# Sinkhorn attention and a residual MLP in one kernel: a later place for the mixed values of batch 1, their round trip through another queue, and several small operations moved

## The chip, the core and the metric

The kernel runs on one core of a Trainium2 chip. The metric is the device time of one execution in microseconds. A core has five engines that run side by side, each through its own list of instructions in order: TensorE (PE, matrix products into PSUM), VectorE (DVE), ScalarE (ACT), GpSimd (POOL) and SyncE (SP), which here only issues DMAs. An instruction waits on semaphores for what it needs; everything behind it on its engine waits too. POOL also issues DMAs. PSUM is handed out in two pools: `psA`, two buffers of two banks, and `psB`, four buffers of one bank.

## What is computed

Inputs are q, k, v of 4 batches, 8 heads, 768 positions and 64 features, a small 8x8 matrix per batch and head, and the MLP's weights. The reference, cut to what matters:

```python
for _ in range(5):                               # on the 8x8 matrices P
    P = softmax over rows; P = P / column sums
k_sorted = einsum("bhij,bhjcd->bhicd", P, k_b)   # k, v cut into 8 blocks of 96 positions
v_sorted = einsum("bhij,bhjcd->bhicd", P, v_b)
attn = softmax(q_b @ k_sorted_b.T / 8)           # each block of q against its own mixed block
x = attn @ v_sorted_b                            # as [4, 768, 512]
a1 = alpha1 * x + beta1
u = x + lam * (w_tok @ a1)                       # mixes positions
a2 = alpha2 * u + beta2
out = u + lam * (relu(a2 @ w_ch1) @ w_ch2)       # 512 -> 2048 -> 512
```

## The kernel before

**Order by hand.** Every instruction of the five engines is issued through a wrapper (line 65), so that the profile shows L65 for nearly all, and groups are told apart by tile names. The program order of each engine is the order in which the Python code runs. The main part walks over 4 batches and 2 halves of positions (hf 0, 1). A half has an h part and a c part. The h part has 16 units `h_unit` (four products into one `psB` bank `h_ps`, then a relu on ScalarE into `hTa` or `hTb`). The c part of batch 0 has three `ch_unit`s of 16 products into one `psB` bank `ch_ps`, each in four parts, then VectorE's sum with u and two stores by SyncE; later batches use `ch_pair`, which saves products by adding and subtracting blocks (`sums`, `TWa`, `TWb`). After each h unit and each c part a table `at` is looked up: `put(batch, half, "h" or "c", n, f)` hangs f behind unit or part n. "h9" of half (0, 0) means: behind the tenth unit. Two entries at one place run in the order in which they were put.

**Work hung there for the next batch.** While batch b goes through the MLP, attention of batch b+1 is done in such places:

- `mix_matrix(b)` (line 371) builds the mixing matrices from P: one small product into a bank `repv_ps` and seven small VectorE operations.
- `mix_v(b, n)` mixes a third of the raw values: two products into a `psA` buffer (`mix_ps`), one ScalarE copy into `mixed`. `bounce_v(b)` writes `mixed` to a DRAM scratch `vscr` with two DMAs, `back_v(b)` reads it back turned, on SyncE, into `Vs`, which the products with the attention weights use.
- `mix_k(b, n)` mixes a third of the keys: eight products into `psA` (`kmix_ps`), four ScalarE copies into `kT`.
- `q_turn_late(g)` turns the queries of head pair g of batch 1: 24 small products into two `psB` banks (`q_ps`), one copy into `qT` from each bank.
- `score(b, g, hf)` forms scores in a `psA` buffer (`sc_ps`) and their exp on ScalarE (`et`); `pv` multiplies with the values into a `psA` buffer (`x_ps`), which VectorE divides and writes to `x`.
- `moe_tok(b, kt)` is the product over positions (`tok_ps`, in `psB`), VectorE adds into `u`, ScalarE copies to `u16`. `moe_cross(b, hf)` turns `u16` by three DMA transposes on SyncE into `uT`, and `moe_affine(b, hf)` makes the input `a2T` of the h part from it with four operations, on VectorE in batch 0.
- `block_weights(n)` makes one eighth of the weight differences `TWa`, `TWb` on VectorE, needed from batch 1 on.
- `block_sums` makes the `sums` on VectorE. `scale_weights` scales the second weight matrix there.

**The start.** Up to about 33 us batch 0's attention and the token weights are prepared. `slow(n)` (line 227) issues n dummy products in fp32 on zeros, whose result nobody reads. One stands at line 961 between `pv_first(0)` and `k_turn(0, 2)`. Loads with a change of type go through POOL in the order of the program: the weights W1p and W2p, then raw v, raw k and q of batch 1 (`load_kv`, `load_q`, line 988). `loads(2)` starts on POOL with a small copy `gate` that waits until `back_v(1)` has written `Vs`.

**Lines that the change touches:** 372 (`mix_matrix`), 541 (`q_turn_late`), 589 (`bounce_v`), 961 (`slow`), 1006 to 1008 (`mix_matrix`, `moe_cross`), 1019 to 1024 (batch 1), 1041 to 1046 (scores and pv of batches 2 and 3), 1064 (`block_weights`).

Of the kernel before, what the change touches and what calls it, by code (L numbers as in the profile page):

```python
# [16 lines left out]
def kernel(  # L17
# [56 lines left out]
    dve = Engine(nc.vector)  # L74
    act = Engine(nc.scalar)
    pool = Engine(nc.gpsimd)
    sp = Engine(nc.sync)
# [9 lines left out]
    def psa(shape, dtype, name):  # L87
        return pools["psA"].tile(shape, dtype, name=name, tag="psA")
# [138 lines left out]
    def slow(n, ps=psa):  # L227
        z = wz[:].bitcast(FT)
        out = ps([128, 512], FT, "warm_ps")
        for _ in range(n):  # L230
            pe.matmul(out[:], z[:, 0:128], z.unsqueeze(1).to_broadcast([128, 2, 256]), start=True, stop=True)
# [27 lines left out]
    def q_copy(b, g, ps, half, eng):  # L259
        eng(  # L260
            qT_of[b][:, g, :].rearrange("p (r t) -> p r t", t=12)[:, :, half * 6:half * 6 + 6],
            ps[half].rearrange("p (t r) -> p r t", t=6),
        )
# [83 lines left out]
    def mix_values(b, ps):  # L347
        bank = ps([128, 512], FT, "repv_ps")
        rep = bank[:, 0:NB * NB]
        pe.matmul(  # L350
            rep, ebh[:, b, :, :, :].rearrange("p a h j -> p (a h j)"),
            P16[:].rearrange("p i j -> p (i j)"), start=True, stop=True,
        )
        sel = att.tile([128, NB, NB], FT, name="sel", tag="sel", bufs=2)
        dve.tensor_tensor(
            sel[:], rep.rearrange("p (i j) -> p i j", j=NB),
            mlo[:].unsqueeze(1).to_broadcast([128, NB, NB]), ALU.mult,
        )
        red = bank[:, 64:64 + NB]
        dve.tensor_reduce(red, sel[:], AXX, ALU.add)  # L360
        big = att.tile([128, H, NB], F16, name="bigV", tag="bigV", bufs=2)
        dve.tensor_tensor(
            big[:], mhi[:].unsqueeze(2).to_broadcast([128, H, NB]),
            red.unsqueeze(1).to_broadcast([128, H, NB]), ALU.mult,
        )
        bigV[b] = big
# [2 lines left out]
    bigP = {}  # L369

    def mix_matrix(b):
        mix_values(b, psa)
        big = att.tile([128, 2, H * NB], F16, name="bigM", tag="bigM", bufs=3)
        dve.tensor_tensor(
            big[:], bigV[b][:].rearrange("p h i -> p (h i)").unsqueeze(1).to_broadcast([128, 2, H * NB]),
            mth[:].unsqueeze(2).to_broadcast([128, 2, H * NB]), ALU.mult,
        )
        bigM[b] = big
        bgp = att.tile([128, 2, 2, H4, NB], F16, name="bigP", tag="bigP", bufs=3)
        for th in range(2):  # L380
            dve.tensor_tensor(
                bgp[:, :, th, :, :], bigV[b][:].rearrange("p (g a) i -> p a g i", a=2),
                mth[:, th:th + 1].unsqueeze(2).unsqueeze(3).to_broadcast([128, 2, H4, NB]), ALU.mult,
            )
        bigP[b] = bgp
# [152 lines left out]
    def q_turn_late(g):  # L538
        ps = q_turn(1, g, psb)
        q_copy(1, g, ps, 0, dve.tensor_copy)  # L540
        q_copy(1, g, ps, 1, act.copy)

    gate = const([1, 1], F16, "gate")

# [7 lines left out]
    def mix_v(b, n, eng):  # L552
        if n == 0:
            mixed[b] = att.tile([128, HB, D], F16, name="mixed", tag="qn" if b == B - 1 else "sums", bufs=1 if b == B - 1 else 2)
        ps = psa([128, 2, 512], FT, "mix_ps")
        raw = raw_of[(b, 1)][:].rearrange("p t d -> p (t d)")
        for m in range(2):
            pe.matmul(
                ps[:, m, :], bigM[b][:].rearrange("p a x -> p (a x)"),
                raw[:, n * 1024 + m * 512:n * 1024 + (m + 1) * 512], start=True, stop=True,  # L560
            )
        eng(
            mixed[b][:, n * 16:(n + 1) * 16, :].rearrange("p t d -> p (t d)"),
            ps[:].rearrange("p m f -> p (m f)"),
        )
# [20 lines left out]

    def bounce_v(b):
        for th in range(2):
            pool.dma_start(
                vscr[b, :, th * HB:(th + 1) * HB, :], mixed[b][th * 64:(th + 1) * 64, :, :],  # L590
            )

    def back_v(b):
        sp.dma_start(Vs[0:BLK, :, 0:D], vscr[b].rearrange("x t d -> t x d"))
# [137 lines left out]
    def moe_cross(b, hf):  # L732
        uT = uT_of[(b, hf)] = att.tile([128, CT, 384], F16, name="uT", tag="uT", bufs=2)
        for m in range(3):
            sp.dma_start_transpose(
                uT[:, :, m * 128:(m + 1) * 128], u16_of[b][:, 3 * hf + m, :],
            )
# [220 lines left out]
    moe_start(0)  # L958
    a1_of[0] = moep.tile([128, 8, C], F16, name="a1", tag="a1", bufs=1)
    pv_first(0)  # L960
    slow(1)
    kp2 = k_turn(0, 2, psb)
    kp3 = k_turn(0, 3, psb)
    for g, kp in ((2, kp2), (3, kp3)):
# [29 lines left out]
    def put(b, hf, kind, n, *todo):  # L994
        at.setdefault((b, hf, kind, n), []).extend(todo)
# [7 lines left out]
    for ks in range(NT):  # L1003
        put(0, 0, "h", ks, lambda ks=ks: prep_wtok(ks, 1, psa, (dve.tensor_copy, act.copy)[ks % 2]))
    put(0, 0, "h", 6, lambda: mix_matrix(1))
    put(0, 0, "c", 6, lambda: mix_matrix(2))
    put(0, 0, "c", 7, lambda: mix_matrix(3))
    put(0, 0, "h", 9, lambda: moe_cross(0, 1))
    for g in range(CT):
        put(0, 0, "h", g, lambda g=g: first_affine(0, slice(0, 128), slice(0, NT), slice(g * 128, (g + 1) * 128)))  # L1010
    for m in range(3):
# [3 lines left out]
    for b in range(1, B):  # L1015
        p = b - 1
        if b == 1:
            for n in range(3):
                put(0, 0, "h", 11 + n, lambda n=n: mix_v(1, n, act.copy))
                put(0, 0, "c", 3 + 3 * n, lambda n=n: mix_k(1, n, (act.copy,) * 4))  # L1020
            put(0, 0, "h", 13, lambda: bounce_v(1))
            put(0, 0, "c", 1, lambda: back_v(1))
            for g in range(H4):
                put(0, 0, "c", (5, 7, 8, 10)[g], lambda g=g: q_turn_late(g))
            put(0, 0, "c", 11, lambda: loads(2))
            seq = [("s", 0), ("s", 1), ("s", 2), ("p", 0), ("s", 3), ("p", 1), ("p", 2), ("s", 4), ("p", 3), ("s", 5),
                   ("p", 4), ("s", 6), ("p", 5), ("s", 7), ("p", 6), ("p", 7)]
            for at_, (kind, n) in enumerate(seq):
                put(0, 1, "h", at_, (lambda n=n: score(1, n // 2, n % 2, psa)) if kind == "s" else (lambda n=n: pv(1, n // 2, n % 2)))
        else:  # L1030
            for n in range(3):
                put(p - 1, 1, "c", (n if b == 2 else 1 + n), lambda b=b, n=n: mix_v(b, n, act.copy))
            for n in range(3):
                put(p - 1, 1, "c", ((2, 5, 7), (4, 7, 10))[b - 2][n], lambda b=b, n=n: mix_k(b, n, (act.copy,) * 4))
            put(p - 1, 1, "c", b, lambda b=b: bounce_v(b))
            put(p - 1, 1, "c", (4 if b == 2 else 7), lambda b=b: back_v(b))
            for kt in range(NT):
                put(*((0, 1, "h", 13) if b == 2 else (1, 0, "c", 1)), lambda b=b, kt=kt: q_cross(b, kt))
            if b + 1 < B:
                put(p, 0, "h", 3, lambda b=b: loads(b + 1))  # L1040
            for (kind, n), at_ in zip(
                pairs, ((0, "h", 0), (0, "h", 2), (0, "h", 4), (0, "h", 6), (0, "h", 9), (0, "c", 0), (0, "c", 4), (1, "h", 2)),
            ):
                for i in range(2):
                    f = (lambda b=b, n=n + i: score(b, n // 2, n % 2, psa)) if kind == "s" else (lambda b=b, n=n + i: pv(b, n // 2, n % 2))
                    put(p, *at_, f)
            for at_ in ((0, "h", 5), (0, "h", 6), (0, "h", 10), (0, "h", 11), (1, "h", 0), (1, "h", 1), (1, "h", 3), (1, "h", 4)):
                put(p, *at_, flush_one)
        if b == 1:
            put(p, 1, "h", 15, flush)  # L1050
        put(p, 1, "h", 3, lambda b=b: moe_start(b))
        for kt in range(3):
            put(p, 1, *(("c", 3) if b == 1 else ("h", 9 + 2 * kt)), lambda b=b, kt=kt: moe_tok(b, kt, psb))
        put(p, 1, *(("c", 3) if b == 1 else ("h", 13)), lambda b=b: moe_cross(b, 0))
        for ci in range(CT):
            put(p, 1, "c", 8 if b == 1 else 8 + ci, lambda b=b, ci=ci: moe_affine(b, 0, (ci,)))
        for kt in range(3):
            put(b, 0, "h", 2 * kt, lambda b=b, kt=kt: moe_tok(b, 3 + kt, psb))
        put(b, 0, "h", 4, lambda b=b: moe_cross(b, 1))
        put(b, 0, "c", 2, lambda b=b: moe_affine(b, 1))  # L1060

    for g, m in enumerate((10, 11, 12, 12)):
        put(0, 0, "h", m, lambda g=g: scale_weights(g))
    for n, at_ in enumerate(((0, 1, "c", 7),) * 4 + ((0, 1, "c", 9),) * 4):
        put(*at_, lambda n=n: block_weights(n))
    for b in range(1, B):
        for hf in range(2):
# [66 lines left out]
```

## Time and profile before

| what | us |
| --- | --- |
| median of 3 runs (lowest to highest) | 259.27 (258.84 to 259.41) |
| the profiled execution | 259.36 |
| its span, first to last instruction | 257.6 |
| PE busy | 244.5 |
| DVE busy | 171.8 |
| ACT busy | 157.0 |
| POOL busy | 47.2 |

A busy TensorE is not TensorE at its peak: the ends of its products are modelled. In a timeline row stand the start, the duration, the engine, the operation, what is written from what, the shape, the number of instructions merged, and in brackets the idle time before, with what ended it. Rows of SyncE are issues; a DMA lands later.

The stages of TensorE in this execution: the h part of half (0, 0) ends at 54.9, its c part at 70.4; the h part of half (0, 1) ends at 86.0; the h part of batch 1 begins at 102.9, that of batch 2 at 158.6, that of batch 3 at 210.7.

### The profile page before, as it was taken

Reading aid. Unit: us, or ns where it says so; the run is one execution under the profiler, and the core shown is the slowest. Engines: PE = TensorE matmul, PEld = TensorE weight load, DVE = VectorE, ACT = ScalarE, POOL = GpSimd, SP = SyncE. Lnnn points to the kernel's source line nnn. Section 1 sums busy time; section 2 is a strip of 40 time slices with the busy share of each in tenths; the row PEclk is TensorE's granted clock in tenths of the full one; section 3 lists DMA queues with packets and bytes.
Section 4 is the critical chain, followed back from the end, with each engine's and each line's share of the span. In section 5 each row is a group of like instructions: output and inputs, shape, how many; then the busy total and the mean of one; then the engine's idle time right before and its main releaser. Section 6 shows DMA issues by size and latency. Waiting matters only on the chain.

```text
span 257.6 us, 6061 instructions
## 1 busy us (share of the span) xinstructions
PE 244.5 (95%) x2418; PEld 158.9 (62%) x2418; DVE 171.8 (67%) x457; ACT 157.0 (61%) x289; POOL 47.2 (18%) x72
## 2 busy tenths in 40 slices
PE   6789999899899999999999999999999999999993
PEld 2366665455455545456865787557756875686783
DVE  5694587654639955759896775298887863462773
ACT  4697675467798688496655587877465004837400
POOL 8598804010091010082000010000000000000000
PEclk9999999999999999999999999999999999999999
DMA  5999999997989976989991259910302232111023
GB/s 92 190 211 208 208 204 210 215 158 182 182 168 182 143 171 125 175 155 175 150 136 46 43 152 133 167 23 0 84 0 45 61 103 63 20 41 43 0 84 81
DMA packets 61936, 31.09 MB, mean 121 GB/s; under 512 B 50562, under 2 KB 57618, under 8 KB 61908
## 3 DMA queue, kind: packets, MB, share of 16 engines
q0 software_dynamic: 21136, 17.70, 44.5%
q1 hardware_dynamic: 40676, 12.97, 30.6%
q8 instruction: 19, 0.31, 0.5%
q14 instruction: 9, 0.07, 0.1%
q10 hardware_dynamic: 96, 0.03, 0.1%
HBM read 32.79 MB, written 8.65 MB: 161 GB/s over the span
## 4 chain that ended last, share of the span: by engine, by line
PE 66%; DMA 15%; DVE 10%; POOL 3%; issue 2%; ACT 2%; DVEq 0%; POOLq 0%
PE h_ps L65 26%; PE tok_ps L65 8%; PE px L65 8%; DMA raw<-in_v_dram 7%; PE ch_ps L65 6%; PE pz L65 5%; PE py L65 5%; DMA W1p<-in_moe_w_ch_dram 5%; DMA v<-in_v_dram 3%; DVE x L65 2%; PE x_ps L65 2%; PE sc_ps L65 2%; DVE ost L65 2%; DVE sums L65 2%; PE mix_ps L65 2%
## 5 line engine op out<-in xcount | busy, mean ns | idle before, releaser
L65 PE MATMUL h_ps<-a2T,W1p 128*128 128x384 bf16 x512 | 93.3, 326 | 0.3 <-DVE a2T L65 0.3
L65 PEld LDWEIGHTS <-W1p 128*128 128x128 bf16 x512 | 47.9, 98 | 31.3 <-issue 0.2
L65 ACT ACTIVATE hTa<-h_ps 128x384 f16<-128x384 f32 x64 | 31.3, 492 | 30.5 <-PE h_ps L65 29.3
L65 ACT ACTIVATE hTb<-h_ps 128x384 f16<-128x384 f32 x64 | 31.2, 490 | 7.5 <-PE h_ps L65 7.5
L65 DVE SCALAR_TENSOR_TENSOR u<-tok_ps,x 128x512 f32<-128x512 f32 x21 | 14.5, 691 | 25.5 <-PE tok_ps L65 25.5
L65 PE MATMUL tok_ps<-a,w_tokT 128*128 128x512 f16 x126 | 30.3, 379 | 0.0
L65 ACT CAST kT<-kmix_ps 64x512 f16<-64x512 f32 x36 | 25.7, 714 | 6.4 <-PE kmix_ps L65 5.9
L65 ACT CAST u<-u 128x512 f16<-128x512 f32 x21 | 13.0, 618 | 21.3 <-DVE u L65 21.2
L65 ACT ACTIVATE et<-sc_ps 96x768 f16<-96x768 f32 (+2 forms) x36 | 24.6, 743 | 1.7 <-PE sc_ps L65 1.7
L65 PEld LDWEIGHTS <-sums 128*128 128x128 f16 x216 | 21.1, 98 | 3.7 <-issue 0.6
L65 PEld LDWEIGHTS <-hTa 128*128 128x128 f16 x192 | 18.3, 98 | 6.7
L65 PEld LDWEIGHTS <-hTb 128*128 128x128 f16 x200 | 18.4, 98 | 5.9
L65 PEld LDWEIGHTS <-w_tokT 128*128 128x128 f16 x126 | 12.3, 98 | 13.1 <-issue 0.2
L65 DVE TENSOR_TENSOR x<-x_ps,rcb 96x512 f16<-96x512 f32 x24 | 16.5, 687 | 0.8
L65 DVE TENSOR_TENSOR sums<-hTa,hTb 128x512 f16<-128x512 f16 (+2 forms) x27 | 8.9, 330 | 10.3 <-ACT hTb L65 10.0
L65 PEld LDWEIGHTS <-et 96*128 96x128 f16 (+4 forms) x288 | 12.0, 100 | 2.6
L65 DVE SCALAR_TENSOR_TENSOR ost<-px,u 128x256 f32<-128x256 f32 x27 | 11.3, 417 | 3.4 <-PE px L65 3.4
L65 POOL DMA_DIRECT2D vscr<-mixed x6 | 3.3, 556 | 55.9 <-ACT mixed L65 55.9
L65 PE MATMUL x_ps<-Vs,et 96*128 96x65 f16 (+4 forms) x288 | 12.8, 195 | 0.0
L65 ACT CAST mixed<-mix_ps 128x1024 f16<-128x1024 f32 x9 | 9.1, 1013 | 5.3 <-PE mix_ps L65 5.2
L65 PE MATMUL ch_ps<-W2p,hTb 128*128 128x512 f16 x48 | 11.8, 379 | 0.0
L65 PE MATMUL ch_ps<-W2p,hTa 128*128 128x512 f16 x48 | 11.7, 379 | 0.0
(140 smaller groups left out, 360.9 us busy)
## 6 DMA issues: line engine op xcount, KB each, us to landing
out_dram<-ost SPq DMA_DIRECT2D x23, 192.0 KB, 2.7
raw<-in_v_dram POOLq DMA_DIRECT2D x6, 384.0 KB, 6.7
raw<-in_k_dram POOLq DMA_DIRECT2D x6, 384.0 KB, 9.7
vscr<-mixed POOLq DMA_DIRECT2D x6, 384.0 KB, 6.1
Vs<-vscr SPq DMA_DIRECT2D x3, 768.0 KB, 8.2
W1p<-in_moe_w_ch_dram POOLq DMA_DIRECT2D x4, 512.0 KB, 11.1
W2p<-in_moe_w_ch_dram POOLq DMA_DIRECT2D x4, 512.0 KB, 14.6
qn<-in_q_dram POOLq DMA_DIRECT2D x12, 128.0 KB, 11.1
```

The costliest lines, as they stand in the source:

```text
L65: ins = getattr(self.eng, name)(*args, **kwargs)
```

## The change

Seven edits.

1. The dummy product `slow(1)` at line 961 is taken out.
2. The mixed values of batch 1: `mix_v(1, n)` goes from h11, h12, h13 to h13, h14, h15 of half (0, 0), `bounce_v(1)` from h13 to h15, `back_v(1)` from c1 to c2.
3. `bounce_v(1)` is issued by SyncE instead of POOL (batches 2 and 3 stay on POOL). `moe_cross(0, 1)`, which is on SyncE too, goes from h9 to c0 and so stands behind the bounce.
4. Both copies of a late q turn are on VectorE (one was on ScalarE), and the four turns go from c5, c7, c8, c10 to c4, c5, c7, c8.
5. `mix_matrix` takes its bank from `psB` instead of `psA`. For batches 2 and 3 it goes from c6 and c7 of half (0, 0) to h1 and h2 of half (0, 1).
6. `block_weights` goes from c7 (four) and c9 (four) of half (0, 1) to c4 (three), c5 (three) and c6 (two).
7. Where two scores of batches 2 and 3 hang behind one h unit, the second goes one unit further. Scores that hang in the c part, and all `pv`, stay.

```diff
     def mix_matrix(b):
-        mix_values(b, psa)
+        mix_values(b, psb)
...
         q_copy(1, g, ps, 0, dve.tensor_copy)
-        q_copy(1, g, ps, 1, act.copy)
+        q_copy(1, g, ps, 1, dve.tensor_copy)
...
     def bounce_v(b):
         for th in range(2):
-            pool.dma_start(
+            (sp if b == 1 else pool).dma_start(
...
     pv_first(0)
-    slow(1)
     kp2 = k_turn(0, 2, psb)
...
-    put(0, 0, "c", 6, lambda: mix_matrix(2))
-    put(0, 0, "c", 7, lambda: mix_matrix(3))
-    put(0, 0, "h", 9, lambda: moe_cross(0, 1))
+    put(0, 1, "h", 1, lambda: mix_matrix(2))
+    put(0, 1, "h", 2, lambda: mix_matrix(3))
+    put(0, 0, "c", 0, lambda: moe_cross(0, 1))
...
-                put(0, 0, "h", 11 + n, lambda n=n: mix_v(1, n, act.copy))
+                put(0, 0, "h", 13 + n, lambda n=n: mix_v(1, n, act.copy))
...
-            put(0, 0, "h", 13, lambda: bounce_v(1))
-            put(0, 0, "c", 1, lambda: back_v(1))
+            put(0, 0, "h", 15, lambda: bounce_v(1))
+            put(0, 0, "c", 2, lambda: back_v(1))
             for g in range(H4):
-                put(0, 0, "c", (5, 7, 8, 10)[g], lambda g=g: q_turn_late(g))
+                put(0, 0, "c", (4, 5, 7, 8)[g], lambda g=g: q_turn_late(g))
...
+                split = kind == "s" and at_[1] == "h"
                 for i in range(2):
...
-                    put(p, *at_, f)
+                    put(p, *at_[:2], at_[2] + (i if split else 0), f)
...
-    for n, at_ in enumerate(((0, 1, "c", 7),) * 4 + ((0, 1, "c", 9),) * 4):
+    for n, at_ in enumerate(((0, 1, "c", 4),) * 3 + ((0, 1, "c", 5),) * 3 + ((0, 1, "c", 6),) * 2):
         put(*at_, lambda n=n: block_weights(n))
```

## The prediction

> **What bounds the kernel now.** I read the page's busy shares, then TensorE's waits, then the timelines around each wait.
>
> ```profile
> PE 244.5 (95%) x2418; PEld 158.9 (62%) x2418; DVE 171.8 (67%) x457; ACT 157.0 (61%) x289; POOL 47.2 (18%) x72
> ...
> PEclk9999999999999999999999999999999999999999
> ```
>
> TensorE is busy 244.5 of 257.6 us at the full granted clock, so a saving must either remove TensorE work or close one of its gaps. The list of what TensorE waited for (left out: five waits of the start, and 0.3 at 33.91 that no edit touches):
>
> ```profile
> PE mix_ps L65 <- DMA raw<-in_v_dram: 1.1, 1, 1.1
> PE q_ps L65 <- ACT qT L65: 1.0, 1, 1.0
> PE sc_ps L65 <- DVE x L65: 0.7, 2, 0.4
> ...
> PE sc_ps L65 <- ACT et L65: 0.5, 2, 0.3
> PE sc_ps L65 <- DVE kT L65: 0.4, 1, 0.4
> ...
> PE px L65 <- DVE ost L65: 0.2, 1, 0.2
> ```
>
> Read: waiter, releaser, us in total, times, longest. Together 3.9 us. The timelines place them (start, duration, in brackets the idle before):
>
> ```profile
> 20.66 1.47 PE L65 MATMUL warm_ps<-wz 128*128 128x512 f32 x2
> 22.07 0.94 PE L65 MATMUL k_ps<-bigK,k 64*64 64x64 f16 x48
> 23.40 0.52 PE L65 MATMUL sc_ps<-qT,kT 64*128 64x96 f16 x16 [0.39 <-DVE kT L65]
> ...
> 50.54 0.60 PE L65 MATMUL mix_ps<-raw,bigM 128*128 128x512 f16 x2 [1.09 <-DMA raw<-in_v_dram]
> ...
> 66.30 0.57 PE L65 MATMUL q_ps<-ident,q8b 64*64 64x64 f16 x24 [1.01 <-ACT qT L65]
> ```
>
> The profiled execution took 259.36 us: span 257.6 and 1.76 around it; it lies 0.09 above the median of the runs, 259.27. Sums below are made against 259.36.
>
> **1. slow(1) removed.** The dummy product holds TensorE from 20.66 to 22.07. Without it `k_turn(0, 2)` starts at about 20.7 and `k_turn(0, 3)` ends near 21.9 (its second bank is free when the exp that ends at 21.41 is done). The next score needs VectorE's `k_copy`, and VectorE is in the `x` product of `pv_first(0)` from 21.04 to 22.00. So that copy starts at 22.00 instead of 22.70, and the score at 22.7 instead of 23.40: 0.70 of the 1.41 us is gained, and TensorE idles 0.8 instead of 0.39. Up to 49 us everything on TensorE, VectorE and ScalarE follows in order; the weights do not hold it (the first W1p piece is issued at 19.0 and takes 10.0, to 29.0; its user, `h_ps` at 33.13, moves to 32.4).
>
> **2. Values of batch 1 two units later (h11..13 to h13..15).** The second raw v load is issued at 31.78 and takes 18.7 us: it lands at 50.50. The DMA engines move 200 to 217 GB/s throughout, so I leave that time where it is. TensorE had finished its earlier work at 49.45; less 0.70 that is 48.75. It now does h12 (0.65), `first_back(2)` (0.43) and h13 (0.65) first, up to 50.48, so it meets the landing within 0.1. After that come three mixes (0.43 each) and two units: 2.6, so the channel products start at 53.13 instead of 54.89. **Gain 1.76**: 1.09 of wait and 0.67 of part 1. Without part 1 it would be 1.09.
>
> **3. Bounce on SyncE, transposes behind it.** ScalarE's three `mixed` copies (1.01 each, with a 0.37 relu between) end at 55.02 before. They start from the same 50.5 and end at about 55.0 again, since ScalarE paces them. So the bounce leaves no earlier than its old 55.31. What changes is SyncE's queue: `moe_cross(0, 1)` is now behind it.
>
> ```profile
> 52.09 3.91 SPq L65 DMA_TRANSPOSE uT<-u  x3
> 62.50 0.36 SPq L65 DMA_DIRECT2D Vs<-vscr  x1
> ...
> 94.59 3.57 SPq L65 DMA_TRANSPOSE uT<-u  x1
> ```
>
> Two issues of about 0.4 (the `Vs` row; POOL's took 0.55) put the transposes at 56.1, 57.4 and 58.7, at their old pitch of 1.3: 4.0 us later than before. Call T the landing of the last. Neither a bounce on SyncE nor a transpose behind one is in this trace, so bounds: low, 58.7 + 2.4, the least landing of a `uT` transpose, 61.1; high, the first issue is held 3.57 as at 94.59, where stores and a bounce were in flight, and the landing is the largest, 4.2: 65.3. I take the median landing on the page, 4.0: **T = 62.7**.
>
> Who waits: `moe_affine(0, 1)` at c6 is first in VectorE's list there, ahead of the sum of channel unit 1 and both copies of q group 2. TensorE is not affected by c4 and c5. But q group 3 at c8 needs two of four banks; unit 2 holds one, so one must come back from group 2. From T: four affines 1.16, the sum 0.60, one copy 0.55 = 2.31. TensorE reaches c8 at 53.13 + nine parts of 0.865 + two key mixes of 0.45 + three turns of 0.50 + some 0.3 in changes between them = 63.6. **New wait: 62.7 + 2.31 - 63.6 = 1.4**; 0 at the low bound, 4.0 at the high one. In the kernel before, the transposes hid under loads and landed long before 63.63, where the affines started without a wait: that cover is what is given up.
>
> The Trainium skill, page "DMA: Bandwidth & Descriptors", section "Two DMAs through the same engine are not ordered", says that within one queue of a DMA engine descriptors start in order. That speaks against this edit: the transposes' data would start only behind the bounce's. By the same page's fit of 2.0 us plus bytes over 436 GB/s the 768 KB bounce would drain by about 59.1 (an estimate), three transposes at the 1.3 pitch would end at 63.0, and the sum would be 257.4 instead of 257.1; no run so far shows the bounce on SyncE.
>
> `back_v` stands behind the transposes (issued up to 59.9) and waits for the bounce: at POOL's 4.1 to 6.5 it goes at 60 to 62, not later than the old 62.50. It takes 8.2, so V is there by 70.2; the first `pv` (74.26 before) needs it at about 72.5. `loads(2)`, gated on it, is no later either. POOL loses two issues of 0.55; nobody waits for them.
>
> **4. q copies on VectorE, at c4, c5, c7, c8.** The old wait at 66.30 is for ScalarE's copy at 65.76, stuck behind four key casts:
>
> ```profile
> 62.86 2.88 ACT L65 CAST kT<-kmix_ps 64x512 f16<-64x512 f32 x4 [0.50 <-PE kmix_ps L65]
> 65.76 0.48 ACT L65 CAST qT<-q_ps 128x384 f16<-128x384 f32 x1
> ```
>
> **It goes: -1.01.** Four copies of 0.55 join VectorE, which has long idle stretches there (3.31 before 58.60, 1.95 before 61.24). Group 0 is needed at 57.9, its load lands at 41.9 + 14.1 = 56.0; groups 2 and 3 land at 58.2, needed at 62. If the bounce beside them delays these by its own 2 us, it still fits.
>
> **5. mix_matrix: psb, and batches 2 and 3 at h1, h2 of the next half.** The same TensorE work (0.13 each), moved. Its seven small VectorE operations (some 1.4 us each time) fall into VectorE's idle 3.38 before 74.72. Zero; if that cover were gone, 0.1 to 0.3.
>
> **6. Differences (block_weights) at c4 to c6.** Eight subtractions, 4.9 us, stood between the channel sums:
>
> ```profile
> 105.80 0.68 DVE L65 SCALAR_TENSOR_TENSOR ost<-ch_ps,u 128x512 f32<-128x512 f32 x1
> 106.40 0.68 DVE L65 SCALAR_TENSOR_TENSOR u<-tok_ps,x 128x512 f32<-128x512 f32 x1
> ...
> 107.12 0.62 ACT L65 CAST u<-u 128x512 f16<-128x512 f32 x1 [2.67 <-DVE u L65]
> 107.64 1.50 ACT L65 ACTIVATE et<-sc_ps 96x768 f16<-96x768 f32 x2
> ```
>
> The token sum ran at 106.40 though its product ended at 105.0; ScalarE idled 2.67 and its exps were late: TensorE's 0.20 and 0.35 (page: 0.5). They now fill VectorE's idle 3.21 before 99.22; the sum runs at once. **Gain 0.55.** Late next: the sum at 99.22 by 1.7, for which only a store waits.
>
> **7. Second scores one unit behind.** The two waits of 0.36 (114.69, 169.42) are for a bank that VectorE frees; a unit of 0.65 covers them. At 169 I count 0.30. At 114 nothing: VectorE is busy without a gap from 112.27 to 124.84, and TensorE already waits 0.21 for it at 124.89; that wait would grow instead. **Gain 0.30.**
>
> **Sum:** 259.36 - 1.76 - 1.01 + 1.4 - 0.55 - 0.30 = **257.1**.
>
> **Rivals.**
> A. No new wait: T at 61.1. For it: by 58.2 the loads are over, so transposes meet less traffic than at 52 to 58. 257.1 - 1.4 = 255.7. It holds up to T = 61.3.
> B. Slower: the transposes don't move until the bounce has landed. Place: SyncE's queue at 55.3. Price: a bounce landing of 6.5 (its largest row) after the second issue at 55.7 is 62.2; three transposes in 3.91 give T = 66.1, a wait of 4.8, and 260.5. For it: the 3.57 row. Against it: there, engines were full of other traffic too. It turns slower from T = 64.9, where the wait eats the 3.62 gained.
> C. The change does less than it says: part 1 gives nothing (a bank or `x` comes later than I read), or group 3 gets both banks of group 2 (one more copy, 0.5). 257.1 + 0.67 to 1.2 = 257.8 to 258.3.
>
> **How the numbers follow.** Forecast 0.46, A 0.24, B 0.20, C 0.10. A measurement of this kernel tells apart about 0.2%, 0.5 us. Forecast, A and C are faster but for 0.03; B covers waits from 3 us on, of which I give 0.05 to no change and 0.15 to slower: 0.77, 0.08, 0.15. The range runs from A with another 0.4 (parts 5 to 7 all saved), 255.3, to B at the 3.57 row, a wait of 4.0, 259.7; outside lie about 0.05 below and 0.12 above.
>
> **What would show it.** Right: the mix starts by 50.6 with h13 behind it, channel products start near 53.1, no wait on ScalarE's `qT`, one on VectorE's `qT` near 63.6 of 0.3 to 3 us with `a2T` before it late; scores near 107 and 168 without a gap, a longer `px` wait on `ost` near 122. Wrong: no gap at q group 3 (A), SyncE's transposes issued past 60 (B), a score later than 23.0 or a granted clock under 1.00 after 20 us (C), or raw v landing past 51.

## The result, and the profile after

| | before | after |
| --- | --- | --- |
| median of 20 runs each (lowest to highest), us | 259.00 (258.62 to 260.03) | 260.28 (258.47 to 262.41) |
| ratio after to before, 95% interval | | 1.0048 [1.0032, 1.0063] |
| profiled execution, and its span | 259.36, 257.6 | 260.25, 258.5 |

The change makes the kernel slower by about half a per cent, against a forecast of 257.1. The runs after also lie further apart, 3.9 us instead of 1.4. (Ratios here leave out executions more than 1.5% above the fastest of their kernel, so where a kernel scatters widely, the medians are given too.)

The page after: the span, the busy shares, the granted clock in 40 slices, and the queue that brings the engines their instructions (packets, MB, share of time).

```profile
span 258.5 us, 6052 instructions
...
PE 243.8 (94%) x2416; PEld 158.2 (61%) x2416; DVE 173.5 (67%) x461; ACT 155.4 (60%) x285; POOL 46.0 (18%) x70
...
PEclk9999999999999999999999999999999999999998
...
q8 instruction: 19, 0.31, 0.5%
```

TensorE is busy 0.7 us less (the dummy product held it for 1.47), and the span is 0.9 longer: idle time was added. The list of TensorE's waits after (waiter, releaser, us in total, times, longest) shows where:

```profile
PE q_ps L65 <- DVE ost L65: 2.3, 1, 2.3
...
PE k_ps L65 <- ACT et L65: 1.4, 1, 1.4
PE x_ps L65 <- issue: 1.3, 1, 1.3
...
PE px L65 <- DVE ost L65: 0.5, 1, 0.5
PE sc_ps L65 <- ACT kT L65: 0.4, 1, 0.4
```

Four old waits are gone as intended: for raw v (1.1), for ScalarE's `qT` (1.0), and the scores' waits for `x` (0.7) and `et` (0.5). In their place stand 2.3 for `ost`, 1.4 at a key turn, 1.3 for "issue", and 0.4 for `kT`. Cut into stages by TensorE's own marks, the two profiled executions compare so (us):

| stage of TensorE | before | after | difference | forecast |
| --- | --- | --- | --- | --- |
| start to first `v_ps` | 14.15 | 13.12 | -1.03 | 0 |
| to the score of group 2 | 9.25 | 9.45 | +0.20 | -0.70 |
| to the first h product | 9.73 | 11.10 | +1.37 | 0 |
| h part of (0, 0) | 21.76 | 20.38 | -1.38 | -1.06 |
| c part of (0, 0) | 15.55 | 16.90 | +1.35 | +0.39 |
| h part of (0, 1) | 15.60 | 16.44 | +0.84 | 0 |
| c part of (0, 1) | 16.88 | 16.89 | 0 | 0 |
| batch 1 | 55.64 | 55.16 | -0.48 | -0.55 |
| batch 2 | 51.94 | 52.04 | +0.10 | -0.30 |
| batch 3 to the end | 47.1 | 47.0 | -0.1 | 0 |

The forecasts of the h part of (0, 0) and of the c part are steps 2 and 3 + 4. The first row is for the most part a difference in when q landed (TensorE's wait for it was 2.3 before and 1.6 after); no edit touches it.

**The start.** TensorE's timeline after (start, duration, and in brackets the idle before):

```profile
19.68 0.21 PE L65 MATMUL k_ps<-bigK,k 64*64 64x64 f16 x1
21.26 0.94 PE L65 MATMUL k_ps<-bigK,k 64*64 64x64 f16 x47 [1.37 <-ACT et L65]
22.57 0.52 PE L65 MATMUL sc_ps<-qT,kT 64*128 64x96 f16 x16 [0.37 <-DVE kT L65]
...
28.60 0.93 PE L65 MATMUL x_ps<-Vs,et 128*128 128x65 f16 x21 [1.31 <-issue]
```

TensorE does one of 48 turning products and then stands for 1.37 us. The list names ScalarE's `et`, but that work ends at 17.34 + 3.08 = 20.42 by this row:

```profile
17.34 3.08 ACT L65 ACTIVATE et<-sc_ps 128x768 f16<-128x768 f32 x6
```

so it can't have held TensorE to 21.26. What fits is the instruction queue: TensorE has 2416 products and as many weight loads, and 19 packets of 16 KB make some 64 bytes for each and 256 in a packet. One packet arrives from 18.83 to 19.77 and the next from 26.10 to 27.03; TensorE goes on 1.48 and 1.57 us after their ends. Before, such a packet came from 19.12 to 20.07, and the halves of the dummy product started 0.78 apart instead of 0.53, with a weight load idle 0.59 on "issue" between them: the dummy product covered the stop. e6 tests this reading. The other profiles bear it out by a count: in all 14, 706 or 707 products and weight loads lie ahead of this stop, whether it falls into the key turn, the dummy product or (e6) a score, and the product behind it starts 1.3 to 1.6 us after the packet's end. The later stop has 962 or 963 ahead of it wherever it shows, 256 further on.

**The new wait at q group 3.** SyncE's issues, VectorE and TensorE there (rows of SP are issues):

```profile
55.73 1.13 SPq L65 DMA_DIRECT2D vscr<-mixed  x2
57.04 3.11 SPq L65 DMA_TRANSPOSE uT<-u  x1
60.20 2.22 SPq L65 DMA_TRANSPOSE uT<-u  x1
62.46 1.27 SPq L65 DMA_TRANSPOSE uT<-u  x1
63.84 0.53 SPq L65 DMA_DIRECT2D Vs<-vscr  x1
```

```profile
65.07 1.25 DVE L65 TENSOR_SCALAR a2T<-uT,ab2col 128x384 bf16<-128x384 f16 x4 [3.07 <-DMA uT<-u]
66.24 0.68 DVE L65 SCALAR_TENSOR_TENSOR ost<-ch_ps,u 128x512 f32<-128x512 f32 x1
66.84 1.01 DVE L65 CAST qT<-q_ps 128x384 f16<-128x384 f32 x2
```

```profile
66.97 0.19 PE L65 MATMUL q_ps<-ident,q8b 64*64 64x64 f16 x1 [2.29 <-DVE ost L65]
67.44 0.54 PE L65 MATMUL q_ps<-ident,q8b 64*64 64x64 f16 x23 [0.28 <-DVE qT L65]
...
72.36 0.34 PE L65 MATMUL sc_ps<-qT,kT 64*128 64x96 f16 x7 [0.44 <-ACT kT L65]
```

The bounce leaves at 55.73, and the first two transposes behind it hold SyncE for 3.11 and 2.22 instead of 1.2. The last lands at 65.07, VectorE stands for it with the channel sum and the q copies behind, and TensorE waits 2.29 + 0.28. In the packet records of this trace the bounce's 128 packets of 6 KB run from 56.87 to 61.08, and the first 256-byte packet of the transposes starts at 59.98, when 118 of the 128 have started: behind the bounce the transposes' data did not move either. The 0.44 ahead of the first score, for a key cast of ScalarE, is not of this wait: it stands in e2, e3, e5, e7, e9 and e11 too, which don't have the wait, and in neither before, e4 nor e12. So it comes with edits 2, 4 or 5; which one wasn't tried.

### The profile page after: what moved, and what is told of

Its sections match the earlier page's. It is cut to its first block, busy times and chain, and to the rows that moved or that the text cites. A ratio compares the mean times of both kernels' runs of the same rounds, so it can differ in the third digit from the quotient of the medians.

```text
span 258.5 us, 6052 instructions
## 1 busy us (share of the span) xinstructions
PE 243.8 (94%) x2416; PEld 158.2 (61%) x2416; DVE 173.5 (67%) x461; ACT 155.4 (60%) x285; POOL 46.0 (18%) x70
## 4 chain that ended last, share of the span: by engine, by line
PE 75%; DVE 9%; ACT 7%; DMA 3%; issue 2%; SPq 1%; POOL 0%; DVEq 0%; POOLq 0%
PE h_ps L65 29%; PE tok_ps L65 11%; PE px L65 8%; PE ch_ps L65 6%; PE pz L65 5%; PE py L65 5%; DMA q<-in_q_dram 2%; PE x_ps L65 2%; PE sc_ps L65 2%; ACT et L65 2%; DVE x L65 2%; DVE sums L65 2%; PE mix_ps L65 2%; DVE a2T L65 1%; PE kmix_ps L65 1%
## 5 line engine op out<-in xcount | busy, mean ns | idle before, releaser
L65 PE MATMUL h_ps<-a2T,W1p 128*128 128x384 bf16 x512 | 94.4, 326 | 0.3 <-DVE a2T L65 0.3
L65 PEld LDWEIGHTS <-W1p 128*128 128x128 bf16 x512 | 47.3, 98 | 30.4
L65 ACT ACTIVATE et<-sc_ps 96x768 f16<-96x768 f32 (+2 forms) x36 | 25.2, 747 | 1.7 <-PE sc_ps L65 1.7
L65 PEld LDWEIGHTS <-kT 64*128 64x128 f16 (+1 forms) x256 | 6.4, 95 | 8.5 <-issue 4.4
## 6 DMA issues: line engine op xcount, KB each, us to landing
raw<-in_k_dram POOLq DMA_DIRECT2D x6, 384.0 KB, 10.2
```

The costliest lines, as they stand in the source:

```text
L65: ins = getattr(self.eng, name)(*args, **kwargs)
```

## The experiments

Each ratio is to executions of the kernel before made alongside; their median was 259.61 (e1 to e4), 259.65 (e5 to e8) and 259.21 (e9 to e12), against 259.00 beside after. So medians of different groups compare to some 0.6 us only.

| run | median (lowest to highest), us | runs | ratio to before |
| --- | --- | --- | --- |
| e1 after with `slow(1)` | 260.24 (259.24 to 262.04) | 10 | 1.0044 [1.0018, 1.0069] |
| e2 after, transposes not behind the bounce | 258.70 (256.50 to 261.16) | 12 | 0.9938 [0.9909, 0.9966] |
| e3 e1 and e2 together | 259.63 (257.54 to 262.06) | 12 | 1.0005 [0.9972, 1.0038] |
| e4 before without `slow(1)` | 259.22 (258.71 to 260.36) | 12 | 1.0001 [0.9984, 1.0017] |
| e5 e2 with the q transposes split | 257.24 (256.38 to 258.56) | 7 | 0.9911 [0.9879, 0.9943] |
| e6 after, instructions moved by 64 | 262.29 | 1 | not measured |
| e7 before with edits 2, 4, 5, 6, 7 | 259.74 (257.93 to 261.72) | 12 | 1.0005 [0.9973, 1.0036] |
| e8 after, the wait filled with work | 259.47 (258.74 to 260.58) | 12 | 1.0003 [0.9982, 1.0024] |
| e9 e5 with `slow(1)` | 257.68 (256.90 to 264.84) | 12 | 0.9934 [0.9909, 0.9960] |
| e10 e7 with the q transposes split | 258.53 (256.70 to 266.91) | 12 | 0.9936 [0.9906, 0.9965] |
| e11 after, bounce on POOL | 259.54 (258.13 to 262.24) | 12 | 1.0011 [0.9982, 1.0041] |
| e12 before with edits 6, 7 | 259.00 (258.54 to 259.84) | 12 | 0.9986 [0.9965, 1.0008] |

### e1 and e4: the dummy product, put back and taken out alone

```diff
     pv_first(0)
+    slow(1)
     kp2 = k_turn(0, 2, psb)
```

e4 is the kernel before without that line.

> The changed kernel with the dummy product slow(1) put back (edit 1 undone, all else as changed). Theory (the removal bought nothing, since TensorE then stands in the next turn of keys until its instructions have arrived, and it opens a second such wait near 28 us and lowers the granted clock in some runs): about 1 us below the changed kernel, 259.2, with a narrow spread and the granted clock near 1.00 in all runs, and the wait of 1.3 us near 28 gone. Rival (the dummy product is as dear as its 1.4 us, or part of it, as the prediction had it): 0.7 above the changed kernel, 261.0. Rival (it changes nothing either way): 260.3.

> The kernel before with only slow(1) taken out (edit 1 alone). Theory (TensorE waits for its instructions in its place, and for the raw v load later): between no change and 1.3 us slower, 259.0 to 260.3, with a granted clock below that of the kernel before in some runs. The prediction's step, 0.7 us gained up to 49 us and then lost again in the wait for raw v, gives no change either, 259.0, but with the score near 22.7 and a wait of 1.8 us for raw v; so the trace must tell them apart.

e4 changes nothing: 1.0001 [0.9984, 1.0017]; a gain of 0.70 us would be 0.9973. e4's waits show the time given back:

```profile
PE mix_ps L65 <- DMA raw<-in_v_dram: 1.5, 1, 1.5
PE k_ps L65 <- ACT et L65: 1.2, 1, 1.2
```

The stop of 1.2 at the key turn appears as soon as the dummy product goes, and what was gained would end in the wait for raw v, as the prediction had it (1.09 to 1.5). So e4's time can't say what the removal is worth ahead of that wait; its trace says a little: the score of group 2 comes 9.32 after the first `v_ps`, not some 8.6 as forecast. One thing more differs: six of e4's twelve executions have a mean granted clock of 0.993 or less, five of the 33 of before beside it, and e4's profile has 3.41 us at 0.50 from 22.6 on, behind this stop. e1 missed its expectation, 259.2: by then I thought the lost cover of the code wait to be the main loss, and it isn't. In e1's profile the dummy product has 0.85 of "issue" inside it, the stop at the key turn is gone and the one near 28 us is 0.21, yet the median stays at 260.24 (ratio 1.0044 against 1.0048), since the wait at q group 3 is there, and a second effect with it. e1's page, and windows behind that wait (bounds, width, busy time of PE, PEld, DVE, ACT, POOL, granted clock, DMA share, GB/s):

```profile
PEclk9999999999589999999999999999999999999999
```

```profile
66.00:68.00 2.00, 1.17 (x25) 0.92 (x25) 1.57 (x4) 0.00 (x0) 0.00 (x0) 0.53 1.66 135
68.00:70.00 2.00, 2.00 (x10) 1.00 (x9) 0.91 (x2) 0.00 (x0) 0.00 (x0) 0.50 1.68 132
70.00:72.00 2.00, 2.00 (x9) 0.92 (x8) 0.00 (x0) 1.43 (x3) 0.18 (x1) 0.50 0.93 259
```

```profile
68.00:70.00 2.00, 2.00 (x16) 1.15 (x16) 1.02 (x2) 0.57 (x1) 0.00 (x0) 1.00 1.68 133
```

The first three windows are of e1, the last of after. After a wait of 2.4 the granted clock falls to 0.50 for 6.8 us in e1 (66.1 to 72.9); in after, behind a wait of 2.3, it stays at 1.00. (The windows hold different products, so their counts aren't compared.) From the first h product to the h part of (0, 1) e1 takes 40.14 us and after 37.28: the fallen clock costs another 2.9 on top of the same wait, of which the next stage gives 0.7 back (15.78 against 16.44).

### e2: the transposes back ahead of the bounce

```diff
-    put(0, 0, "c", 0, lambda: moe_cross(0, 1))
+    put(0, 0, "h", 9, lambda: moe_cross(0, 1))
```

> The changed kernel with the transposes of half 1 (moe_cross(0, 1)) back at h9, so ahead of the bounce in SyncE's queue; the bounce stays on SyncE at h15. Theory (the new wait of TensorE at q group 3, 2.3 + 0.3 us, is for the late landing of these transposes): the wait goes, 2.5 us below the changed kernel, 257.8. Rival (the wait moves on to the banks or to VectorE's copies, since both copies of a turn are on VectorE now): 0 to 1 below, 259.3 to 260.3, with a wait on VectorE's qT still there.

The wait at q group 3 is gone, and the h part of (0, 1) starts at 67.16 instead of 70.95. But the h part of batch 1 starts at 103.40, not 100.5, and the time is 258.70 where 257.8 was expected. TensorE and then VectorE of e2 there:

```profile
98.93 1.89 PE L65 MATMUL ch_ps<-W2p,hTb 128*128 128x512 f16 x8
103.40 1.19 PE L65 MATMUL h_ps<-a2T,W1p 128*128 128x384 bf16 x4 [2.58 <-DVE a2T L65]
```

```profile
102.97 1.25 DVE L65 TENSOR_SCALAR a2T<-uT,ab2col 128x384 bf16<-128x384 f16 x4 [3.80 <-DMA uT<-u]
```

Of 3.8 us gained at 67 only 0.9 is left at 103, at full clock in both up to there. A second chain ends here. SyncE of e2, and behind it POOL and SyncE singly:

```profile
84.60 12.13 SPq L65 DMA_TRANSPOSE qT<-qn  x6
96.82 1.00 SPq L65 DMA_DIRECT2D out_dram<-ost  x2
97.91 3.81 SPq L65 DMA_TRANSPOSE uT<-u  x3
```

```profile
89.17 1.10 POOL L65 DMA_DIRECT2D vscr<-mixed  x2 [8.97 <-ACT mixed L65]
```

```profile
92.30 4.43 SPq L65 DMA_TRANSPOSE qT<-qn  x1
```

The chain: bounce of batch 1, its way back (issued at 62.94), V's landing, `gate` and `loads(2)` on POOL, the landing of batch 2's queries by 84.6, their six transposes on SyncE, and behind these the `uT` transposes for batch 1. It starts when the bounce has landed, not when TensorE is ready. With TensorE 3.8 earlier, the bounce of batch 2 (89.17) now leaves while the q transposes are being issued, and the last two of them take 2.36 and 4.43 instead of 1.2. In the trace of before the six took 7.73 and were done at 92.09, and the bounce left at 91.43: its hold fell on the first `uT` transpose, the 3.57 at 94.59 that the prediction shows, and still `a2T` came (102.23) just in time for TensorE at 102.92.

Behind e2's wait the clock is at 0.50 for 3.4 us (105.1 to 108.5), and e2's runs lie from 256.5 to 261.2. By medians of all its executions e2 is 0.35% faster than before.

### e3: transposes ahead of the bounce, with the dummy product

> Both of the last two: slow(1) back and the transposes ahead of the bounce. Theory: the two add up, 3.5 us below the changed kernel, 256.8, faster than the kernel before by about 2. Rival (one of them hides the other): as the better of the two alone, 257.8.

Expected 256.8, measured 259.63: a miss. The wait for `a2T` is there again, 2.29, with the h part of batch 1 at 103.50. So e2's wait is not of its start, and a saving ahead of 100 us ends in the chain whatever made it.

### e11: the bounce alone back on POOL

```diff
-            (sp if b == 1 else pool).dma_start(
+            pool.dma_start(
```

Here `moe_cross` keeps its place at c0, but nothing of the bounce is in SyncE's queue, so the transposes go when `u16` is there.

> The changed kernel with the bounce of batch 1 issued by POOL again, all else as changed, so the transposes stay at c0 but nothing large stands ahead of them in SyncE's queue. Theory (the issue of the transposes, 3.1 and 2.2 us instead of 1.2 in the changed kernel, is held by the bounce ahead of them): they are issued from 54.5 on at the 1.3 pitch, land near 60, and TensorE's wait at q group 3 is gone or below 0.3; then the chain of the second experiment holds, 258 to 259. Rival (their place at c0 is what makes them late, wherever the bounce is): the wait stays over 1.5 us, 260.3.

```profile
62.03 0.57 PE L65 MATMUL q_ps<-ident,q8b 64*64 64x64 f16 x24
...
63.49 0.83 PE L65 MATMUL q_ps<-ident,q8b 64*64 64x64 f16 x24
```

Group 3 runs at 63.49 without a wait. The transposes were issued from 49.70 to 54.74, ahead of the bounce (54.88) and not from 54.5 on as expected. That is the undoing of one part alone, so standing behind the bounce in SyncE's queue is the cause of the 2.3. What a bounce of another queue would do to transposes at that place isn't tested by it. The chain of e2 takes the saving again: a wait of 2.48 for `a2T` at 103.44, and 259.54 in the median.

### e8: the wait filled with dummy products

```diff
     def q_turn_late(g):
+        if g == 3:
+            warm(9)
```

> The changed kernel with nine dummy products of 512 columns, about 2 us, ahead of the fourth late q turn, so that TensorE works in most of the stretch in which it waits there for VectorE. Theory (a wait of over 2 us lets the granted clock fall to half in some runs, which costs about 1.7 us more each time, and this makes the changed kernel's spread): granted clock near 1.00 in all runs, highest run below 260.6, median 259.5. Rival (the clock has no part): median and spread as the changed kernel, 260.3, 258.5 to 262.4, or 0.5 more where the dummies overrun the wait.

The nine products (2.11 us, no reader) stand where TensorE waited. The h part of (0, 1) starts 5.88 behind the landing of the transposes (69.94 and 64.06), as in after (70.95 and 65.07), so nothing is taken off the path. Yet the ratio to before falls from 1.0048 to 1.0003 and the runs close up to 258.74 to 260.58, with no slice of the page below full clock. The mean granted clock of each execution points the same way (a block of 3.41 us at 0.50 in 258 us makes 0.993, an estimate). Of the 20 of after, five have 0.997 or more, and their median is 259.12; nine have 0.990 to 0.993, median 260.31; six have 0.987 or less, median 261.54. Of e8's twelve, eight have 0.998 or more. So after at full clock takes about as long as before, and the 1.2 us between 259.12 and its median of 260.28 goes with the clock; e8, which has the wait's length but not its idleness, gives about as much back (0.8 by medians, 1.2 by ratios).

The clock is not the only thing that scatters: the five at full clock lie from 258.47 to 260.25, and those of e3 and e7 from 257.5 to 261.1. Nor does every fall come from this wait: in e4 and e6 it stands behind the stop for instructions, and without the dummy product six of twelve (e4), three of seven (e5) and four of twelve (e8) have 0.993 or less, against five of 33 (before, beside e4), one of twelve (e9) and two of twelve (e12) with it. So the product may also keep the clock up; these counts are small, and e4's and e5's executions at the lower clock are not longer.

The Trainium skill, page "TensorE: Matmul & The Clock Gate", "HAM oscillation — how this bites in real kernels", gives the rule that TensorE should not idle for more than some 3.4 us. By that rule a wait of 2.3 would cost nothing beyond itself; here waits of 2.36 (e1), 2.58 (e2), 2.29 (e3), 2.48 (e11), 1.74 (e6) and 1.19 (e4) went with half clock, and the measurement decides. Its section "What's actually happening" has the clock judged in free-running windows of 3.4 us, and with this the traces agree: the stretches at 0.50 last 3.41 (e2, e3, e11, e4), 6.83 (e1) and 10.24 (e6), and fall in some executions only.

### e6: 32 tiny products ahead of the start

```diff
     slow(2)
+    tiny(32)     # out[:, 0:4] from wz, nobody reads it
     warm(1)
```

This moves every later instruction of TensorE by 64 places against the blocks of 256, and almost nothing in time (the first `v_ps` is at 13.14, in after at 13.12).

> The changed kernel with 32 tiny products (four columns each, on zeros, result unread) added among the first dummies, so that everything on TensorE lies 64 instructions later in its program. Theory (in the changed kernel TensorE waits for instructions at the second product of the key turn and at the third values product, since its instructions come in blocks and the next block has not arrived): both waits move about 64 instructions earlier, into the score or values product before the key turn and into the token weights; none is left at the second product of the key turn. Rival (it waits there for ScalarE's exp, as the list of waits has it): the wait of 0.6 to 1.4 us stays at the second product of the key turn. Time as the changed kernel within its spread, 259 to 262.

```profile
18.30 0.38 PE L65 MATMUL sc_ps<-qT,kT 64*128 64x96 f16 x9
20.42 0.34 PE L65 MATMUL sc_ps<-qT,kT 64*128 64x96 f16 x7 [1.74 <-issue]
20.69 1.13 PE L65 MATMUL x_ps<-Vs,et 128*128 128x65 f16 x24
21.75 1.49 PE L65 MATMUL k_ps<-bigK,k 64*64 64x64 f16 x48
...
27.24 0.50 PE L65 MATMUL sc_ps<-qT,kT 64*128 64x96 f16 x8 [0.72 <-ACT et L65]
```

The stop leaves the key turn, where all 48 products now run in one piece, and stands in the middle of the score before it, put down to "issue"; the later one stands ahead of a score too (it was expected in the token weights), and is put down to `et`. From the new place of the first stop to the old one there are 7 scores, 24 products with the values and 1 turning product, 32 products with a weight load each: 64 instructions. A data dependence does not move with the count of instructions; a block of code does. (e6's 262.29 has 10.2 us at a clock of 0.50 from 21.4 on, behind the 1.74.)

### e5, e9, e7, e10: the hidden chain

e5 is e2 with three of the six q transposes of batch 2 behind the `uT` transposes; e9 has the dummy product besides.

```diff
-                put(*((0, 1, "h", 13) if b == 2 else (1, 0, "c", 1)), lambda b=b, kt=kt: q_cross(b, kt))
+                put(*(((0, 1, "h", 13) if kt < 3 else (0, 1, "c", 3)) if b == 2 else (1, 0, "c", 1)), lambda b=b, kt=kt: q_cross(b, kt))
```

> As the second experiment (transposes of half 1 ahead of the bounce), and of the six q transposes of batch 2, which stand on SyncE ahead of the transposes for the first half of batch 1, three go behind them (from h13 of half (0, 1) to c3, after moe_cross(1, 0)). Theory (a second chain of transfers, values of batch 1 out and back, loads of batch 2, its q transposes, then the transposes for batch 1, ends only at 102.9 whatever TensorE does; TensorE ran into it, 2.6 us of wait at 103.4): that wait goes or falls below 0.5, the h part of batch 1 starts near 101, and the time is 2 to 3 us below the second experiment: 256.0 to 256.8. Rival (those transposes wait for something else, ScalarE's u16 or the bounce's traffic): the wait stays, 258.7. Rival (the moved q transposes make the first scores of batch 2 late): a new wait near 105, 257.5 to 259.

> The fifth experiment (transposes of half 1 first, q transposes of batch 2 in two parts) with slow(1) put back. It weighs edit 1 where no later chain takes its effect back. Theory (without slow(1) TensorE gets at most half of its 1.4 us, the rest is a wait for instructions): 0.4 to 0.9 us above the fifth experiment, 257.6 to 258.1. Rival (slow(1) is free): 257.2, the same. Rival (slow(1) keeps the clock up): below 257.

```profile
100.32 0.81 PE L65 MATMUL h_ps<-a2T,W1p 128*128 128x384 bf16 x4
```

The h part of batch 1 of e5 starts at 100.32 without a wait, 2.6 earlier than before. Its median, 257.24, is above the 256.0 to 256.8 expected, but e5 is faster than both kernels, 0.9911 [0.9879, 0.9943], by undoing edit 3's order and freeing the chain. This settles the chain as the cause of e2's, e3's and e11's waits. e9, with the dummy product back, has 0.9934 [0.9909, 0.9960]: the product costs 0.4 us by medians and 0.6 by ratios, but the intervals overlap, and no difference is shown.

e7 and e10 are the kernel before with edits 2, 4, 5, 6 and 7; e10 adds the split of the q transposes.

> The kernel before with edits 2, 4, 5, 6 and 7: slow(1) stays, the bounce stays on POOL, the transposes stay at h9. Theory (edits 2 and 4 save 2.1 us up to 86 us, and the chain of transfers that ends near 102.5 takes them back in a wait of TensorE for a2T; edits 6 and 7 save about 0.6 behind it): 258.4, with that wait in the trace, about 2 us. Rival (the bounce on SyncE is what makes that chain late): no such wait, 256.2.

> The kernel before with edits 2, 4, 5, 6, 7 and the split of the q transposes: bounce on POOL, transposes at h9, slow(1) stays. It weighs edit 3. Theory (the bounce on SyncE lands no earlier, 63 against 62.4, since the loads and transposes set its pace, and is worth nothing): as the ninth, within 0.5 us, 257.1 to 258.1. Rival (the bounce on SyncE helps): 1 us above the ninth.

e7 has the h part of (0, 1) at 67.52, 2.9 earlier than before, and the same chain gives back most of it: 1.3 is left at 101.62, with 0.61 of wait for `a2T` (some 2 was expected). The profiled execution took 258.10; in the median nothing is left, 259.74 (257.93 to 261.72), and what separates the two wasn't followed. With the split, e10 reaches 0.9936 in seven of its executions, as e9 (0.9934), so the bounce on SyncE is worth nothing by itself; five others took 265.3 to 266.9. e10's profile is one of these:

```profile
PE h_ps L65 <- ACT a2T L65: 4.6, 1, 4.6
```

Its windows show the DMA engines at 13 GB/s from 116 to 120 us, with eight loads of batch 3 and three transposes issued, where e9 has 223 GB/s; a `uT` transpose issued by 114.5 is waited for until 130.56. What stalled there wasn't followed, and whether e9's single 264.84 is the same stays open too.

### e12: differences and scores alone

e12 is the kernel before with edits 6 and 7.

> The kernel before with edits 6 and 7 alone (differences at c4 to c6, second scores one unit later). Theory and prediction: the waits of 0.20 and 0.35 near 108 and of 0.36 near 114 and 169 go, the wait for ost near 124 grows by about 0.3: 0.6 to 0.9 us gained, 258.5 to 258.9 where the kernel before has 259.3. Rival (VectorE's saturated stretch from 112 to 125 takes all of it back): within 0.2.

0.9986 [0.9965, 1.0008]: 0.36 us in the middle where the prediction had 0.85, and not shown to differ from no change. e12's profile says where: batch 1 takes 55.12 (before 55.64), but batch 2, where only edit 7 acts, 52.05 (before 51.94). The rows have the reason. Two scores and two h units, undivided in before (first) and split in after (second):

```profile
160.60 0.51 PE L65 MATMUL sc_ps<-qT,kT 64*128 64x96 f16 x16
161.05 1.48 PE L65 MATMUL h_ps<-a2T,W1p 128*128 128x384 bf16 x8
162.36 0.81 PE L65 MATMUL tok_ps<-a,w_tokT 128*128 128x512 f16 x3
```


```profile
106.32 0.34 PE L65 MATMUL sc_ps<-qT,kT 64*128 64x96 f16 x8
106.59 0.82 PE L65 MATMUL h_ps<-a2T,W1p 128*128 128x384 bf16 x4
107.35 0.34 PE L65 MATMUL sc_ps<-qT,kT 64*128 64x96 f16 x8
107.62 0.82 PE L65 MATMUL h_ps<-a2T,W1p 128*128 128x384 bf16 x4
108.28 1.46 PE L65 MATMUL tok_ps<-a,w_tokT 128*128 128x512 f16 x6
```

From the first score to the token product it is 1.96 split, against 1.76 undivided, with the same products (the same pair of batch 3 in after, at 161.48, takes 1.97). So a split pair costs 0.2, by its two more changes between the kinds; three pairs per batch cost some 0.6, more than the 0.36 of wait that they remove in batch 2. That it is the changes is read from these rows; no run varied their number alone.

## Why the prediction was wrong, step by step

**What bounds the kernel** was read rightly as far as it went: TensorE with 3.9 us of gaps. What was missed is that a second chain, through SyncE and POOL, ends within 0.7 us of TensorE at 103 (`a2T` starts at 102.23, TensorE's product at 102.92). It shows no wait before, so reading only waits can't find it.

**Step 1** failed in its reason: 0.70 gained was put at the score of group 2, and that stage grew by 0.20. The dummy product lay in the shadow of a stop for TensorE's own instructions. The step looked at what data the next products need and not at the 0.78 between the halves of the product. What the removal is worth stays open. The pair of profiles compared here is one draw of a stage that scatters with the packet's arrival: with the dummy product it takes 9.25 to 10.46 (seven profiles, median 9.74), and 9.25 is before's; without it 8.70 to 9.45 (six, e6 left out, median 9.12). So some 0.6 may be won there after all, but nothing of it arrives (e4: no change) while a later wait takes it. The later stop, 1.31 of the stage to the first h product, can't be put down to this edit: it is 1.31 in after, 1.04 in e2, 0.76 in e5, 0.49 in e11 and not listed in e4 and e8, all without the dummy product, and 0.21 to 1.30 in e1, e3, e7, e9 and e10 with it.

**Step 2** was right in its mechanism: the mix ran without a wait, and the stage lost 1.38 where 1.06 was forecast (20.4 in every profile with the edit at full clock). The other 0.3 is no listed wait. It adds nothing to the sum by itself, as its saving ends in the chain unless that is freed.

**Step 3** failed in its size, and this is the term that turned the sign: e2, which takes only this back, is faster than before (0.9938). T was put at 62.7 with bounds of 61.1 to 65.3; it was 65.07. The wait was put at 1.4 and measured 2.57, although TensorE came to group 3 at 64.68 and not at 63.6. The error: two issues held, 3.11 and 2.22, where none was taken at the forecast's middle and one at the upper bound. The last transpose was therefore issued at 62.46 and not at 58.7 (0.9 of this is the first one's later start, 57.04 for 56.1); its landing, 2.6 for the 4.0 assumed, gave 1.4 back. Rival B had the mechanism: transposes that don't move on behind a bounce, slower from T = 64.9; its sign, an issue past 60, is in the trace. It was given 0.20. Its own T, 66.1, was too high by 1.0, and its price of 260.5 is close to the measured 260.28 partly by luck, since it has neither the chain nor the clock. The same trace held the row that should have weighed more, a `uT` transpose at 94.59 with a bounce in flight, held 3.57. As for the rule that data of one queue starts in order, cited there: the packets agree (59.98 for the transposes' first, 56.87 for the bounce's), but the estimate of 63.0 for the last landing is 2.1 below the measured one; the bounce drained at 61.08 and not by 59.1. The fit behind that estimate is given on the page for DMAs issued by GpSimd, and this bounce was issued by SyncE. That `back_v` and `loads(2)` are no later failed as well: `back_v` went at 63.84 where 60 to 62 was put, V landed at 71.5 where 70.2 was put, and the q transposes of batch 2 began at 85.67 (84.36 before). Above all the step asked only whether this path becomes later, and not whether a gain on TensorE can get past it.

To the wait came what no step had: the clock, some 1.2 us in the median, and 0.44 at the first score for `kT`, a term of edits 2, 4 or 5 that was put at nothing.

**Step 4** was right: ScalarE's wait is gone, and without the bounce edit group 3 ran at 63.49 (e11), against a forecast of 63.6. **Step 5** was right: two products of 0.13 left the c part of (0, 0) and are in the h part of (0, 1). **Step 6** fits (-0.48 in the stage against -0.55), though step 7 acts in that stage too and e12 doesn't separate them there. **Step 7** failed: the waits went and the `px` wait grew as foreseen (0.21 to 0.55), but the changes of kind, put at nothing, cost more than the waits had. Batch 2 takes 52.04 to 52.06 in all twelve profiles with the edit and 51.94 in before and e4: 0.1 longer where 0.30 shorter was forecast.

The profiled execution of after was at full clock all but its end. Measured less forecast, by the table of stages: start up to the first h product +1.24, h part -0.32, c part +0.96, h part of (0, 1) +0.84, batch 1 +0.07, batch 2 +0.40, the end -0.1. That is 3.1 and leads from 257.1 to its 260.2. The rows are not independent: group 3 follows the landing of the transposes, so what TensorE lost at the start came out of its wait there. The start's share is also the least certain: the first h product comes at 32.48 to 33.85 in after, e2, e5, e9 and e11 alike, with the dummy product or without. The median has less of that scatter and more of the clock.

## What to carry to other kernels

Before a gap on the bounding engine is closed, look for the chain that arrives next at the following junction, also where it causes no wait yet: here some 3 us were won at 67, and half to all of it lost at 103, in four kernels (e2, e3, e7, e11), until a queue order there was changed as well. Here a DMA transpose issued while other transfers were in flight, of its own queue or another, often held the issuing engine, so price such a move by the issue time in the busy row of the trace, not in the quiet one. A wait on TensorE can cost more than its own length, as the clock may follow; and a dummy product that nobody reads can be lying over a stop for code, so take it out alone first, and compare more than one profile.

## What the runs showed of the hardware that was not expected

- The granted clock fell to 0.50 at waits of 1.19 (e4) to 2.58 us (e2), in some executions and in blocks of 3.41 us (3.41, 6.83, 10.24).
- TensorE stood 0.7 to 1.4 us at the key turn, and 1.7 at a score (e6), for a block of its own instructions, with loads running at about 180 to 210 GB/s (that it is the block is shown by e6's shift, by the same count of instructions ahead of it in all profiles and by the packets' times, not by a record of the fetch), and the list of waits put it to another engine in six of them (`et`, which in after had ended 0.8 us earlier).
- Behind or beside a bounce in flight, the first transpose took 2.4 to 3.8 us to issue in all profiles that were read for it (before, after, e1 to e5, e7 to e12) and the next 1.2 to 4.4, against 1.2 in quiet stretches. A bounce isn't needed: with loads alone in flight, the third of three took 1.7 to 2.8 (e2, e3, e5, e7, e10, e11, near 53), while in before, at 52.09, all three took 1.2 to 1.3. What decides it isn't known.
- Two more changes between score and h products cost 0.2 us (1.96 against 1.76 with the same products).
